# Attention and expert router on one core: the first pair of heads prepared in two halves, an overflow region moved into a product, the last product in two column parts

## The chip, the cores and the metric

The kernel runs on one core of a Trainium2 chip. The metric is the device time of one execution in microseconds (us); the number given for a kernel is the median of its runs. TensorE (PE in the profile) multiplies, VectorE (DVE), ScalarE (ACT) and GpSimd (POOL) work on elements, SyncE (SP) issues DMAs. Each engine executes its own instructions in order, and waits on semaphores for the others.

## The reference

There are two blocks, and the second takes the output of the first.

```python
# attention: q, k, v are (4, 8, 768, 64), centroids (8, 16, 64)
q_assign = argmax(normalised q . normalised centroids)      # 16 clusters
k_assign = argmax(normalised k . normalised centroids)
mask = q_assign[..., :, None] == k_assign[..., None, :]
scores = where(mask, q @ k.T / 8, -1e9)
x = softmax(scores) @ v                                     # then (3072, 512)
# router: expert_emb (8, 512), w1 (8, 512, 1024), w2 (8, 1024, 512)
logits = normalised x @ normalised expert_emb.T / tau
e = argmax(logits); gate = softmax(logits)[e]
out = gate * (relu(x @ w1[e]) @ w2[e])                      # each row by its own expert
```

## The kernel before

**Attention.** The 4 x 8 heads are taken as 16 pairs of heads (`NP`), with the two heads of a pair side by side in 128 partitions. A pair has 12 units: two halves of the queries (`hq`) by six blocks of 128 keys (`j`). `scores` (L497) makes a unit's scores in psum in two parts. Part 1 is the f32 product of `kT` and `qT`; part 0 is a bf16 product of the one-hot table `hot` (`t["H"]`), which adds a large negative number where the clusters differ. `expo` (L526) is ScalarE's exponential into one of six `prob` buffers, and `attend` (L531) multiplies by v and lets VectorE add up the sums. In the loop over units (L1441) TensorE scores two units ahead of the two that it attends.

Each pair is prepared by pieces (L365). "turn" brings q and k into the layout with the head's columns in partitions; "products" multiplies by the centroids (L411) and VectorE transposes the result (L420); "choose" finds the first best cluster with four VectorE instructions (L429 to L432); "codes" writes signed numbers into `cd`; and the table is `cd` transposed. For later pairs the turning is VectorE's and the table is made by a DMA transpose, all while an earlier pair is attended. For the first pair there is nothing to hide behind: `begin` (L327) does the turning on TensorE (L382) with evictions by ScalarE and VectorE (L388, L392), makes the table by twelve TensorE transposes (L466), and fills TensorE with matmuls on ones, `keep_up` (L229), ahead of the first data (ten) and ahead of the table (six). The order of every engine's instructions is the order of the program text; nothing is reordered by a scheduler.

The first loads: ScalarE's queue takes the centroids and the first half of k, SyncE's queue takes q, the rest of k, the embeddings `emb` and `tau`, then v in eight pieces, then the next pair. GpSimd makes the constants (identities, iotas, the zeros of `cd`). `unit_experts` and `turned_experts` scale and transpose `emb`.

**Experts.** After routing, 20 items are worked off: four "early", then "block" (128 rows) and "sized" (all rows of one expert up to a capacity) in turn; `later` holds all but the early ones, and `LAST` is the last of them. A block is `hidden` (L1299, two halves of 512 columns, w1) and `result` (L1318, w2, 16 matmul records of 512 columns in two halves of the contraction), an eviction by ScalarE into one of three buffers `y`, and a scatter by GpSimd. A sized item is `sized_hidden` and `sized_result`. Weights sit in two slots; the next w1 or w2 for a slot is loaded by SyncE when the slot's product is done. Gathers and scatters are queued as jobs and issued by `pump` and `share` in between. Every relu of `hidden` and `sized_hidden` is ScalarE's, in program order with the evictions of y.

`overflow` (L1589) is a region that runs only if some expert's rows exceed all the places planned (`n_used > KX`, L1605). With these inputs it is not taken, but each engine branches at it and adds the counts that the region's work would have added to its semaphores. Before, it stands ahead of item LAST-1:

```python
for i, it in enumerate(later):
    if i == LAST - 1:
        overflow()
        weights1(later[LAST])
        weights2(later[LAST])
```

Of the kernel before, what the change touches and what calls it, by code (L numbers as in the profile page):

```python
# [39 lines left out]
def kernel(  # L40
# [143 lines left out]
    def load(n, names):  # L184
        b, hp = pairs[n]
        t = ld.setdefault(n, {})
        for nm in names:
            x = t[nm] = ldp.tile([P, NJ, 2, D], F32, tag=nm + "32", name=nm + "32")
            for h in range(2):
                rows = {"q": q, "k": k, "v": v}[nm][b, 2 * hp + h]  # L190
                if nm == "v":

                    r = rows.rearrange("(i j a t) d -> a i t j d", i=2, a=2, t=SQ)
                    for g in range(P // SQ):
                        nc.sync.dma_start(
                            out=x[SQ * g : SQ * g + SQ, :, h], in_=r[g // 2, g % 2]
                        )
                    continue
                if n == 0:

                    for i in range(1 + (nm == "k")):
                        js = slice(NJ // 2 * i, NJ // 2 * i + NJ // 2) if nm == "k" else slice(0, NJ)
                        queue = nc.scalar if nm == "k" and i == 0 else nc.sync
                        queue.dma_start(
                            out=x[:, js, h], in_=rows.rearrange("(j p) d -> p j d", p=P)[:, js]
                        )
                    continue


                for w in range(D // SQ):  # L210
                    p0 = D * h + SQ * w
                    nc.sync.dma_start(
                        out=x[p0 : p0 + SQ].rearrange("p j h (o i) -> p (j h o) i", i=SQ),
                        in_=rows.rearrange("(s t) d -> t s d", t=SQ)[:, :, SQ * w : SQ * w + SQ],
                    )
# [36 lines left out]
    def constants():  # L252
        nc.vector.memset(onesb, 1.0)
        keep_up(10, idle_ps[:, 0])
        nc.vector.memset(epsc, EPS)
        make_identity(nc, ident)
        nc.gpsimd.iota(io_i, pattern=[[1, P]], base=0, channel_multiplier=0)

        nc.gpsimd.iota(
            tok_i.rearrange("p (b j) -> p b j", j=NJ),  # L260
            pattern=[[S, B], [P, NJ]],
            base=0,
            channel_multiplier=1,
        )
        for i, (p0, w) in enumerate(((0, -BIG), (D, -2.0))):
            nc.gpsimd.memset(wcd[p0 : p0 + D], w)
        make_identity(nc, identb)
        nc.gpsimd.memset(cd, 0.0)
        for i, (p0, c) in enumerate(((0, -BIG), (D, -1.0))):
            nc.gpsimd.memset(cd[p0 : p0 + D, :, :, 2 - 2 * i : 3 - 2 * i], c)  # L270
        make_upper_triangular(nc, sltb, val=1.0, diag=False)
        for prob in probs:
            nc.gpsimd.memset(prob[:, :, HS:HE], EPS)
        nc.gpsimd.memset(gate_p, 0.0)
        nc.vector.memset(cnB, 0.0)
        nc.vector.memset(ones, 1.0)
        nc.vector.memset(embT, 0.0)
        nc.vector.memset(cumx[:, 0], 0.0)
        nc.vector.tensor_copy(io_b, io_i)
        nc.vector.tensor_copy(io_f, io_i[:, 0:SQ])  # L280
        nc.vector.tensor_scalar(prefc, io_b[:, 0:C], -1.0, float(C), ALU.mult, ALU.add)
        nc.vector.tensor_scalar(prefe, io_b[:, 0:E], -1.0, float(E), ALU.mult, ALU.add)
# [17 lines left out]
    def unit_centroids():  # L300
        unit_rows(cn_r)
        nc.vector.tensor_scalar(cn2, bc(c_sb, [P, 2, D], 1), cn_r, None, ALU.mult)
        bk = misc()
# [8 lines left out]
    def unit_experts():  # L312
        unit_rows(en_r)
        nc.vector.reciprocal(tau, tau)
        nc.vector.tensor_scalar(emb, emb, en_r, tau, ALU.mult, ALU.mult)

    def turned_experts():
        bk = misc()
        for c in range(KD):
            nc.tensor.transpose(  # L320
                bk[:, E * c : E * c + E], emb[:, P * c : P * c + P], ident[0:E, 0:E]
            )
        nc.vector.tensor_copy(
            embT[:, :, 0:E], bk[:, 0 : KD * E].rearrange("p (c e) -> p c e", e=E)
        )

    def begin():  # L327

        nc.scalar.dma_start(out=c_sb, in_=centroids.rearrange("h c d -> (h c) d"))
        load(0, "q")  # L330
        load(0, "k")
        nc.sync.dma_start(out=emb, in_=moe_expert_emb)
        nc.sync.dma_start(out=tau, in_=moe_tau.to_broadcast([E, 1]))
# [4 lines left out]
        nc.scalar.activation(en_r, epsc[0:E], ACTF.Sqrt)  # L338
        norm_rows(cn_r, c_sb, P)
        unit_centroids()  # L340
        piece(0, "turn0")
        piece(0, "turn1")
        norm_rows(en_r, emb, E)

        nc.scalar.activation(cn_r, epsc, ACTF.Exp)
        piece(0, "products")
        for m in range(2):
            scores(m, (1,))
        un[2]["s_ps"] = psO.tile([P, 2, 512], F32, tag="o_ps", name="s_ps2")
        scores(2, (1,))  # L350
        piece(0, "choose")
        piece(0, "codes")
        keep_up(6, misc())
        unit_experts()
        rest = piece(0, "turn_numbers")
        next(rest)
        for m in range(3):
            scores(m, (0,))
        next(rest, None)
        turned_experts()  # L360
        for m in (0, 2, 1):
            expo(m)
        token_numbers()

    def prep_pieces(n):  # L365
# [8 lines left out]
        def turn(nm, half):  # L374
# [12 lines left out]
            if nm == "q":  # L387
                (nc.vector.tensor_copy if half else nc.scalar.copy)(  # L388
                    t["qT"][:, HS * half : HS * half + HS], bk[:, 0:HS]
                )  # L390
            else:
                (nc.scalar.copy if half else nc.vector.tensor_copy)(  # L392
                    in_halves(t["kT"])[:, half], bk[:, 0:HS].rearrange("p (s t) -> p s t", t=SQ)
                )
# [27 lines left out]
        def choose():  # L422
# [3 lines left out]
            amax = smp.tile(shp[0:2], F32, tag="amax", name="amax")  # L426
            sel = smp.tile(shp, BF16, tag="sel", name="sel", bufs=1)
            pm = smp.tile(shp[0:2], BF16, tag="pm", name="pm")
# [6 lines left out]
        def codes():  # L435
            pm = t["pm"]
            nc.scalar.activation(cd[..., 1], pm, ACTF.Copy, scale=wcd)
            for i, p0 in enumerate((0, D)):
                g = slice(p0, p0 + D)
                if n == 0:  # L440
                    nc.vector.scalar_tensor_tensor(
                        out=cd[g, :, :, 2 * i],
# [6 lines left out]
                    continue  # L449
# [4 lines left out]
            if n > 0:  # L454
                nc.sync.dma_start_transpose(
                    out=t["H"], in_=cd.rearrange("p s h c -> p (s h c)")
                )

        def turn_numbers():

            U = S // (4 * SQ)
            bks = []
            for half in range(2):
                bk = misc().bitcast(BF16)
                for u in range(U):
                    nc.tensor.transpose(  # L466
                        bk[:, P * u : P * u + P],
                        cd[:, U * half + u].rearrange("p h c -> p (h c)"),
                        identb,
                    )  # L470
                bks.append(bk[:, 0 : P * U].rearrange("r (s x) -> r s x", x=P))
            H = [t["H"][:, U * half : U * half + U] for half in range(2)]
            nc.vector.tensor_copy(H[0][:, :, 0:SQ], bks[0][:, :, 0:SQ])
            nc.scalar.copy(H[0][:, :, D:], bks[0][:, :, D:])
            nc.vector.tensor_copy(H[1][:, :, 0:SQ], bks[1][:, :, 0:SQ])
            yield
            nc.vector.tensor_copy(H[1][:, :, SQ:], bks[1][:, :, SQ:])  # L477
            nc.vector.tensor_copy(H[0][:, :, SQ:D], bks[0][:, :, SQ:D])

        return {  # L480
            "turn0": lambda: turn_blocks("q") if n else (turn("q", 0), turn("q", 1)),
            "turn1": lambda: turn_blocks("k") if n else (turn("k", 0), turn("k", 1)),
# [3 lines left out]
            "turn_numbers": turn_numbers,  # L486
# [10 lines left out]
    def scores(i, parts=(0, 1)):  # L497
# [10 lines left out]
        for part in parts:  # L508
            if part == 0:
                l = t["H"][:, 2 * j : 2 * j + 2, D:]  # L510
                r = t["H"][:, :, SQ * hq : SQ * hq + SQ]
            else:
# [786 lines left out]
    def hidden(it, halves=(0, 1)):  # L1299

        d = mo[it]
        for half in halves:
            if half == 0:
                d["hT"] = mop.tile([P, F], F32, tag="hT", name="hT")
# [12 lines left out]

    def result(it, halves=(0, 1)):  # L1318
        d = mo[it]
        for half in halves:  # L1320
            if half == 0:
                d["y_ps"] = bank("y_ps", psY)
# [55 lines left out]
    def between(n, it):  # L1378
        b, nb = divmod(n, NHP)
        if n == 0:  # L1380
# [6 lines left out]
            elif it == 3:  # L1387
                later_constants()
        elif it == 0 and n > 1:
# [49 lines left out]
    with tc.manual_schedule(engines=by_hand):  # L1439
        begin()  # L1440
        for i in range(0, len(units), 2):  # L1441
# [8 lines left out]
            for m in range(i + 2 if i else 3, min(i + 4, len(units))):  # L1450
                scores(m)
                expo(m)
                if it == 2 and m == i + 2:
                    piece(n + 1, "codes")
            between(n, it)
# [12 lines left out]
            for m in range(i, i + 2):  # L1468
                attend(m)
            if it == 2:  # L1470
# [10 lines left out]
            if it == 0:  # L1481
# [107 lines left out]
        def overflow():  # L1589
            n_used = nc.values_load(used[0:1, 0:1], min_val=0, max_val=KX + NO)  # L1590
            slot = later[-1].slot

            def more(j0, n):
                for j in range(j0, j0 + n):
                    it = Item("whole", KX + j, slot, more_tables)
# [9 lines left out]
            with tc.If(n_used > KX):  # L1605
# [12 lines left out]
                with tc.If(n_used > KX + MORE[0]):  # L1618
                    more(MORE[0], MORE[1])
                    with tc.If(n_used > KX + MORE[0] + MORE[1]):  # L1620
                        more(MORE[0] + MORE[1], MORE[2])

# [5 lines left out]
        for i, it in enumerate(later):  # L1628
            if i == LAST - 1:
                overflow()  # L1630
# [24 lines left out]
            elif i < LAST:  # L1655
# [10 lines left out]
                result(it)  # L1666
# [5 lines left out]
            else:  # L1672
# [3 lines left out]
                result(it)  # L1676
# [43 lines left out]
```

## Time and profile before

| | us |
|---|---|
| median of three runs (694.60 to 694.82) | 694.73 |
| the profiled execution: its own time | 695.09 |
| its span, first to last instruction | 693.3 |
| TensorE busy in the span | 684.1 |
| first exponential starts at | 14.61 |
| TensorE's work of the last product | 680.62 to 687.65 |
| last eviction of y, last scatter issued at | 687.69, 688.65 |

The mean granted clock of TensorE is 0.999 of full speed. Times inside the profile count from the start of the span. A line of a timeline gives the start, the duration, the engine, the source line and the operation with its tiles and shapes, and in brackets how long the engine had been idle and who released it. A line of the waits gives who waited for whom, the total, how often, and the longest. Matmul ends are modelled, and an f32 matmul appears as two records.

### The profile page before, as it was taken

To read this page: it belongs to the slowest core of one execution; us is meant where nothing else is said; L and a number is where in the kernel's file an instruction comes from. 1 tells how busy PE (TensorE), PEld (TensorE's weight loads), DVE (VectorE), ACT (ScalarE), POOL (GpSimd) and SP (SyncE) were. 2 spreads that over 40 slices of the span, in tenths; PEclk is the share of its full clock that TensorE was granted. 3 is DMA by queue.
4 is the path that set the end of the run, shared out by engine and by line. 5 is a ranking of instruction groups with operands and counts; after the bars stand their busy time and mean duration, and the time that the engine had idled before them with its cause. 6 is when DMAs were issued, how large, how long until landed. Compare 5 with 4: busy or idle time off the path is not lost.

```text
span 693.3 us, 16291 instructions
## 1 busy us (share of the span) xinstructions
PE 684.1 (99%) x6517; PEld 459.3 (66%) x6517; DVE 381.8 (55%) x667; ACT 262.6 (38%) x443; POOL 266.2 (38%) x494
## 2 busy tenths in 40 slices
PE   8999999999999999999999999999999999999996
PEld 4444444444444444455866778888979797979694
DVE  5789898999989999988564122140211303030310
ACT  5666665577656765576224120101010111111111
POOL 2122221321232212343315343576656465646502
PEclk9999999999999999999999999999999999999999
DMA  8755556875577588699699957457777686879450
GB/s 133 123 93 105 101 94 95 155 144 103 106 138 157 99 163 162 182 261 271 176 318 359 353 211 269 136 182 283 281 273 279 205 301 228 301 256 315 155 225 32
DMA packets 244157, 135.55 MB, mean 196 GB/s; under 512 B 207840, under 2 KB 207842, under 8 KB 244076
## 3 DMA queue, kind: packets, MB, share of 16 engines
q1 hardware_dynamic: 237116, 121.10, 64.3%
q0 software_dynamic: 6016, 13.12, 5.4%
q8 instruction: 54, 0.88, 0.6%
q10 hardware_dynamic: 944, 0.23, 0.2%
q14 instruction: 27, 0.22, 0.1%
HBM read 115.92 MB, written 13.12 MB: 186 GB/s over the span
## 4 chain that ended last, share of the span: by engine, by line
PE 91%; issue 3%; DMA 3%; POOL 1%; DVE 1%; POOLq 0%; ACT 0%; DVEq 0%
PE s_ps L518 22%; PE o_ps L540 18%; PE h_ps L1309 10%; PE y_ps L1325 10%; PE h_ps L1220 9%; PE y_ps L1258 6%; PE misc L1258 5%; PE x_ps L1220 3%; DMA out_dram<-ys,spidx 3%; PE misc L590 2%; PE misc L411 2%; PE misc L669 1%; PE idle_ps L232 1%; POOL xin L1078 0%; POOL out_dram L1089 0%
## 5 line engine op out<-in xcount | busy, mean ns | idle before, releaser
L529 ACT ACTIVATE prob<-s_ps 128x768 f32<-128x768 f32 x192 | 154.1, 814 | 100.7 <-PE s_ps L518 99.7
L518 PE MATMUL s_ps<-qT,kT 64*64 64x384 f32 x1536 | 155.6, 482 | 0.0
L540 PE MATMUL o_ps<-prob,v 64*64 64x385 f32 x1536 | 141.1, 483 | 0.0
L559 DVE TENSOR_TENSOR acc<-acc,prob 128x768 f32<-128x768 f32 x128 | 121.7, 951 | 8.5
L540 PEld LDWEIGHTS o_ps<-prob,v 64*64 64x64 f32 x1536 | 58.1, 133 | 65.2 <-issue 57.6
L1309 PE MATMUL h_ps<-xTm,w1s 128*128 128x128 f32 x768 | 88.5, 275 | 0.0
L1309 PEld LDWEIGHTS h_ps<-xTm,w1s 128*128 128x128 f32 x768 | 87.5, 192 | 1.4 <-issue 1.0
L1267 DVE STREAM_TRANSPOSE ys<-y_ps 128x256 f32<-128x256 f32 (+4 forms) x16 | 6.2, 404 | 147.0 <-PE y_ps L1258 119.1
L1325 PE MATMUL y_ps<-w2s,hT 128*128 128x512 f32 x192 | 84.5, 593 | 0.0
L518 PEld LDWEIGHTS s_ps<-qT,kT 64*64 64x64 f32 x1536 | 55.2, 133 | 36.9 <-issue 32.3
L574 POOL COPY behind<-acc 1x1 f32<-1x1 f32 x30 | 6.7, 223 | 178.2 <-DVE acc L559 169.3
L1220 PE MATMUL h_ps<-xTs,w1s 128*128 128x272 f32 (+7 forms) x384 | 72.9, 346 | 1.1 <-ACTq L1605 1.1
L1220 PEld LDWEIGHTS h_ps<-xTs,w1s 128*128 128x128 f32 x384 | 66.6, 190 | 8.0 <-issue 2.4
L1316 ACT ACTIVATE hT<-h_ps 128x512 f32<-128x512 f32 x24 | 14.3, 596 | 149.1 <-PE h_ps L1309 121.5
L1089 POOL DMA_INDIRECT out_dram<-ys,spidx x56 | 56.2, 1004 | 35.5 <-DVE ys L1282 18.3
L518 PE MATMUL s_ps<-hot 64*64 64x384 bf16 x768 | 64.2, 325 | 1.0 <-DVE hot L477 0.7
L1078 POOL DMA_INDIRECT xs<-x_rows,gpidx x56 | 56.9, 1016 | 18.7 <-issue 18.1
L1325 PEld LDWEIGHTS y_ps<-w2s,hT 128*128 128x128 f32 x192 | 35.6, 190 | 40.2 <-issue 39.9
L518 PEld LDWEIGHTS <-hot 64*64 64x64 bf16 x768 | 23.8, 106 | 43.9 <-issue 41.8
L1258 PE MATMUL misc<-hTs,w2o 128*128 128x272 f32 (+7 forms) x256 | 48.2, 346 | 0.0
L1258 PE MATMUL y_ps<-hTs,w2o 128*128 128x272 f32 (+7 forms) x256 | 48.0, 346 | 0.0
L1258 PEld LDWEIGHTS misc<-hTs,w2o 128*128 128x128 f32 x256 | 44.4, 190 | 2.7 <-issue 0.2
(274 smaller groups left out, 711.0 us busy)
## 6 DMA issues: line engine op xcount, KB each, us to landing
w1s<-in_moe_w_dram SPq DMA_DIRECT2D x18, 2048.0 KB
w2s<-in_moe_w_dram SPq DMA_DIRECT2D x18, 2048.0 KB
v<-in_v_dram SPq DMA_DIRECT2D x128, 48.0 KB
k<-in_k_dram SPq DMA_DIRECT2D x62, 96.0 KB
q<-in_q_dram SPq DMA_DIRECT2D x60, 96.0 KB
x_rows<-xb SPq DMA_DIRECT2D x60, 96.0 KB
xr<-x_rows SPq DMA_DIRECT2D x9, 512.0 KB
w1s<-in_moe_w_dram SPq DMA_DIRECT2D x4, 1024.0 KB
```

Of the source, the lines that this page charges most:

```text
L411: nc.tensor.matmul(bk[2 * C * i : 2 * C * i + 2 * C, 0:HS], lhsT=cnB[:, hp], rhs=r, start=True, stop=True,)
L518: nc.tensor.matmul(s_ps[D * half : D * half + D, h, 0:HS], lhsT=l[rows, half], rhs=r[rows], start=part == (1 if len(parts) < 2 else 0), st ...
L529: nc.scalar.activation(d["prob"][:, :, 0:HS], d["s_ps"][:, :, 0:HS], ACTF.Exp, scale=scale)
L540: nc.tensor.matmul(g["o_ps"][D * h : D * h + D, half, 0:HE], lhsT=ld[n]["v"][keys, j, h], rhs=d["prob"][keys, h, 0:HE], start=(j == 0), st ...
L559: nc.vector.tensor_tensor(g["acc"], g["acc"], d["prob"][:, :, 0:HS], ALU.add)
L1078: nc.gpsimd.indirect_dma_start(out=to, out_offset=None, in_=of, in_offset=bass.IndirectOffsetOnAxis(ap=at, axis=0), bounds_check=n - 1, oo ...
L1089: inst = nc.gpsimd.indirect_dma_start(out=to, out_offset=bass.IndirectOffsetOnAxis(ap=at, axis=0), in_=of, in_offset=None, bounds_check=n - 1,
L1220: nc.tensor.matmul(bk, lhsT=w1s[it.slot][:, c, P * f : P * f + P], rhs=d["xT"][:, c, 0:C], start=(c == 0), stop=(c == KD - 1),)
L1258: nc.tensor.matmul(bks[g][:, 0:C], lhsT=d["w2"][:, f, P * g : P * g + P], rhs=d["hT"][:, f, 0:C], start=(f == 0), stop=(f == KF - 1),)
L1309: nc.tensor.matmul(bk[:, m : m + P], lhsT=w1s[it.slot][:, c, f0 + m : f0 + m + P], rhs=d["xT"][:, P * c : P * c + P], start=(c == 0), stop ...
L1316: nc.scalar.activation(d["hT"][:, f0 : f0 + 512], bk, ACTF.Relu)
L1325: nc.tensor.matmul(bk, lhsT=d["hT"][:, P * c : P * c + P], rhs=w2s[it.slot][:, c], start=(c == 0), stop=(c == KF - 1),)
```

## The change

The first pair is prepared in two halves. Half 0 is the first 384 tokens of q and k, enough for units 0 to 2. Its four loads of 96 KB go over both SyncE's queue (head 0) and ScalarE's queue (head 1), those of half 1 over SyncE's; v of this pair is loaded in two pieces in natural order. `emb` and `tau` are loaded through GpSimd, after the first identity. `begin` runs turn, half product, choice, codes and table half by half, interleaved with the scores of units 0, 2 and 1; unit 3 is scored between the first two attends, and the choice product of pair 1 comes after units 4 and 5. Eight filler matmuls remain ahead of the first data, none ahead of the table. Scaling and evicting the embeddings moves to ScalarE, `token_numbers` into pair 0's fifth step. In the expert part, `overflow` moves between the two halves of the second product of block LAST-2; the region's items use that block's weight slot and other buffers, and the region reloads the second half of w2 at its end. The last block's second product is made in two column parts, 384 and 128, each evicted on its own.

```diff
-    def load(n, names):
+    def load(n, names, halves=(0, 1), queue=nc.sync):
...
+                if n == 0:
+                    x_h, rows = x[:, :, h], rows.rearrange("(j p) d -> p j d", p=P)
+                    if nm == "v":
+                        nc.sync.dma_start(out=x_h, in_=rows)
+                        continue
+                    for half in halves:
+                        js = slice(NJ // 2 * half, NJ // 2 * half + NJ // 2)
+                        (queue if h else nc.sync).dma_start(out=x_h[:, js], in_=rows[:, js])
+                    continue
...
-        keep_up(10, idle_ps[:, 0])
+        keep_up(8, idle_ps[:, 0])
         nc.vector.memset(epsc, EPS)
         make_identity(nc, ident)
+        nc.gpsimd.dma_start(out=emb, in_=moe_expert_emb)
+        nc.gpsimd.dma_start(out=tau, in_=moe_tau.to_broadcast([E, 1]))
...
     def unit_experts():
-        unit_rows(en_r)
-        nc.vector.reciprocal(tau, tau)
-        nc.vector.tensor_scalar(emb, emb, en_r, tau, ALU.mult, ALU.mult)
+        nc.vector.tensor_scalar(en_r, en_r, 1e-6, tau, ALU.add, ALU.mult)
+        nc.vector.reciprocal(en_r, en_r)
...
+        for half in range(2):
+            load(0, "qk", (half,), nc.sync if half else nc.scalar)
         load(0, "v")
         load(1, "qk")
         constants()
...
+        nc.scalar.activation(cn_r, epsc, ACTF.Sqrt)
         norm_rows(cn_r, c_sb, P)
+        norm_rows(en_r, emb, E)
         unit_centroids()
...
+        piece(0, "turn", "q", 0)(nc.vector.tensor_copy)
+        piece(0, "turn", "k", 0)(nc.scalar.copy)
+        turned_centroids()
+        unit_experts()
+        nc.scalar.activation(emb, emb, ACTF.Copy, scale=en_r)
+        piece(0, "half_products", 0)
+        piece(0, "turn", "q", 1)(nc.scalar.copy)
+        ld[0]["c_ps"] = psS.tile([P, 2, 512], F32, tag="s_ps", name="c_ps")
+        piece(0, "turn", "k", 1)(nc.scalar.copy)
+        turned_experts()
+        junk = smp.tile([P, 1], F32, name="junk1", bufs=1)
+        nc.scalar.activation(junk, epsc, ACTF.Exp)
+        piece(0, "choose", 0)
+        piece(0, "codes", 0)
+        scores(0, (1,))
+        piece(0, "half_products", 1)
         un[2]["s_ps"] = psO.tile([P, 2, 512], F32, tag="o_ps", name="s_ps2")
         scores(2, (1,))
+        evicts = piece(0, "table", 0)
+        evicts[0](nc.vector.tensor_copy)
+        evicts[1](nc.scalar.copy)
+        scores(0, (0,))
+        expo(0)
+        piece(0, "choose", 1)
+        piece(0, "codes", 1)
+        scores(2, (0,))
+        expo(2)
+        scores(1, (1,))
+        evicts = piece(0, "table", 1)
+        evicts[0](nc.vector.tensor_copy)
+        evicts[1](nc.scalar.copy)
+        scores(1, (0,))
+        expo(1)
...
+        def half_products(half):
+            W = HS // 2
...
+            for i in range(4):
+                r = in_halves(t["qT" if i < 2 else "kT"])[:, i % 2]
+                nc.tensor.matmul(
+                    bk[2 * C * i : 2 * C * i + 2 * C, 0:W],
+                    lhsT=cnB[:, hp],
+                    rhs=r[:, W // SQ * half : W // SQ * half + W // SQ],
+                    start=True,
+                    stop=True,
+                )
...
+            nc.vector.transpose(t["asn"][:, W * half : W * half + W], bk[:, 0:W])
...
+                nc.gpsimd.tensor_scalar(to[..., 1], pm, wcd, None, ALU.mult)
...
+    def result_last(it):
+
+        d = mo.pop(it)
+        y = mop.tile([P, DM], F32, tag="y", name="y", bufs=3)
+        cols = [slice(0, DM - P), slice(DM - P, DM)]
+        for cut in cols:
+            bk = bank("y_ps", psY)
+            for c in range(KF):
+                nc.tensor.matmul(
+                    bk[:, cut],
+                    lhsT=d["hT"][:, P * c : P * c + P],
+                    rhs=w2s[it.slot][:, c, cut],
...
+            nc.scalar.activation(
+                y[:, cut], bk[:, cut], ACTF.Copy, scale=it.gates[:, it.col : it.col + 1]
+            )
+        scatter(out[:], it.tables[2][:, it.col : it.col + 1], y, N)
...
+            elif it == 4:
+                token_numbers()
...
+            if (n, it) == (0, 1):
+                piece(1, "products")
...
                 attend(m)
+                if m == 0:
+                    scores(3, (1,))
+                    scores(3, (0,))
+                    expo(3)
...
-            slot = later[-1].slot
+            own = later[-3]
...
+                own.e = expert_of(own)
+                load_part(w2s[own.slot], moe_w2, own.e, KF, 1, 2)
...
             if i == LAST - 1:
-                overflow()
                 weights1(later[LAST])
                 weights2(later[LAST])
...
-                result(it)
+                result(it, (0,))
+                if i == LAST - 2:
+                    overflow()
+                result(it, (1,))
...
                 hidden(it)
-                result(it)
+                result_last(it)
```

## The prediction

> **What bounds the kernel now.** I read the page from the top, then the chain of waits at the start, the waits around line 1605, and the timeline of the end.
>
> ```profile
> span 693.3 us, 16291 instructions
> PE 684.1 (99%) x6517; PEld 459.3 (66%) x6517; DVE 381.8 (55%) x667; ACT 262.6 (38%) x443; POOL 266.2 (38%) x494
> ```
>
> TensorE is busy for 684.1 of 693.3 us. Its 9.2 us of idleness lie in four places: 1.07 before the first matmul, about 1.4 in gaps between 5.5 and 18 us, 1.10 at line 1605, and 5.65 after the last matmul (687.65). From 30 to 490 us it has none, so time won at the start lasts to the end. Beside the idleness, TensorE does work at the start that no output needs. The chain of waits there (start, length, what):
>
> ```profile
> 1.07 4.45 PE idle_ps L232 x10
> ...
> 5.73 0.93 PE q_ps L382 x6
> ...
> 9.09 0.59 DVE asn L420
> ...
> 13.80 0.38 DVE hot L477
> ...
> 14.20 0.39 PE s_ps L518 x4
> ...
> 16.48 1.60 PE o_ps L540 x15
> 18.07 0.83 PE misc L411 x8
> ```
>
> The first stage is a serial path: load, turn, product, choice on VectorE (9.09 to 12.5), table, and only at 14.61 the first exponential. At 18.07 four units are scored and two attended; I call this the mark. What follows it is the same work before and after. In TensorE's timeline,
>
> ```profile
> 7.14 0.52 PE L382 MATMUL misc<-ident,k 128*128 128x128 f32 x3 [0.17 <-DMA k<-in_k_dram]
> 11.09 1.47 PE L232 MATMUL misc<-onesb 128*128 128x512 bf16 x6
> ```
>
> the first shows that the last part of k arrives just before 7.14, the second 1.47 us of filler while VectorE chooses. At line 1605 the waits of TensorE and SyncE, and the instructions of that line on GpSimd, are:
>
> ```profile
> PE h_ps L1220 <- ACTq L1605: 1.1, 1, 1.1
> SPq L1128 <- PEq L1605: 6.5, 1, 6.5
> ```
> ```profile
> L1605 POOLq EVENT_SEMAPHORE  x5: 17/43/43, 656.7 to 665.4; - x5
> L1605 POOLq INC_SWDGE_SEM  x1: 1230/1230/1230, 665.4 to 665.4; - x1
> ```
>
> TensorE stands 1.10 us because ScalarE first evicts y (0.69 us) and only then passes the region. SyncE issues the last expert's w1 as soon as TensorE is past. GpSimd stays in the region until 666.6: there it waits for every transfer it has issued.
>
> **What the skill says.** "TensorE: Matmul & The Clock Gate", Part 1: the array starts at half clock, and a free-running 3.4 us window of activity raises it. The trace agrees: turns follow 0.213 us apart up to 5.95 and 0.109 us apart from 6.15. "Runtime: NRT & Kernel Launch", Instruction fetch mechanics: a taken branch must fetch its target. The trace has 0.4 us (ScalarE, 655.5 to 655.9) to 0.9 us (VectorE, 643.0 to 643.9) from the branch to the next event. "DMA: Bandwidth & Descriptors", Issuing engines are not separate DMA queues: all issuers share 16 engines. Here the sharing is uneven: GpSimd's gather issued at 630.46 landed at 632.79, but those issued at 634.46 and 638.21, with weight loads in flight, took 6.1 and 6.3 us by the trace's landings.
>
> **Start.** Added: two load DMAs (q and k go as eight of 96 KB, not six), four matmuls in the choice product, five choice instructions, three code writes. Removed: 6 of 8 DMAs of v (5.25 us of SyncE's issue become about 1), eight filler matmuls, one table eviction. Moved: emb and tau from SyncE to GpSimd, expert scaling (0.53) and its eviction (0.19) from VectorE to ScalarE, token numbers (0.84) to a place where VectorE waits 2.83 us (before 29.45).
> 1. Loads. The bytes on each queue are as before. In the trace q of head 0 landed at 3.73 (192 KB on SyncE), ScalarE's two k parts at 4.53 and 6.26. After: q and k of head 0 by 3.7, q of head 1 by 4.5, k of head 1 by 6.2. The filler ends at 1.07 + 8 x 0.427 = 4.5, so q turns to 5.2 at the cold clock, then TensorE waits 1 us. k turns to 6.6, the centroids to 6.8, cnB copies (2 x 0.23) to 7.3. First half product from 7.35 (whole product before: 7.85).
> 2. ScalarE's norm of emb (0.95) stands ahead of the kT copy; free if emb lands by 5.7. GpSimd issues it at about 1.35. An unloaded GpSimd transfer takes 2.3 us (630.46), a loaded one 6.3: 3.7 to 7.6. I take 5.2, since loads of 256-byte packets are only just starting. Behind GpSimd's two DMAs (1.0 each, as its gathers) lie the iotas: VectorE's io_b moves from 1.55 to 3.7, and cn is ready at 5.2 instead of 5.0; hidden by k's arrival.
> 3. Half the choice: 384 columns take 0.55 to 0.58, 24 take 0.17, so 192 take 0.38 to 0.40: transpose 0.40, four steps 1.5, codes 0.55. Product to 7.8, codes ready at 10.35. GpSimd's code product is not in the trace: 0.2 (memset) to 0.85 (L576), beside 0.54 of VectorE: nothing.
> 4. Meanwhile TensorE turns the rest (0.33 + 0.33), experts 0.4, scores of unit 0 (0.65), second half product (0.45), scores of unit 2 (0.65): to 10.65. Table 0.4 to 11.05, ScalarE's eviction 0.48 to 11.55, first exponential at 11.8. ScalarE's table load (1.28) fits from 9.45 to 10.75.
> 5. Second half: choice 11.2 to 12.7, codes 13.25, table 13.7, eviction 14.2, exponential of unit 1 to 15.0. TensorE: unit 1 and attend 0 to 14.55, unit 3 to 15.35, attend 1 to **16.0**. The mark falls from 18.07 to 16.0: **-2.07**. The product of pair 1 (0.83) moves behind units 4 and 5; its codes are due at about 20.8, as unit 6 is.
> What can be lost: if the 1 us gap keeps the array cold through the next window, half-rate work adds 0.5 to 1.0; if emb lands at 7.6, the kT copy goes from 6.7 to 8.5, 1.9 later. What can be won: k at 5.6 gives 0.5. Ends: -2.6 to -0.2.
>
> **Region.** It now stands after eight of the block's sixteen matmul records: 647.85 + 3.51 = 651.36 in old times. TensorE must drain (0.22, as 654.88 to 655.1) and branch (0.4 to 0.9); I take 0.75 in all. ScalarE has nothing pending, so the 1.10 goes: without more, the stage gains 0.35, say 0.4. But the block's y eviction now follows the region. The region's items write the same three y buffers, so this eviction waits for counts that GpSimd adds when it leaves. Behind it in ScalarE's queue are the next item's relus; TensorE has four psum groups (4.45) before it needs the first. GpSimd's last scatter ahead of the region is issued at 652.97. Before, it landed at 655.14 in quiet; now SyncE issues w1 at 651.65, and its packets begin at 652.8 (before: issue 655.17, packets from 656.4). Landing: 655.1 unloaded, 659.2 as the loaded gathers, 662.3 as the y scatter (655.89 to 665.16). I take 658.5. Leaving takes 0.2 + 1.23, then y 0.69 and a relu 0.3 with handovers 0.2: the fifth group starts 2.6 after the landing, at 661.1, against 660.44 before: **+0.7**. Bounds: -0.4 (landing before 657.4) to +4.4. y's own scatter is issued later; nothing before the end waits for it. w1 is issued 3.5 us earlier, w2 as before, and 20 us of slack hide both. The other buffers of the region's items (hTs, psH, the reload of w2's second half) matter only in a branch that isn't taken; the waits that they put on TensorE end with ScalarE's and SyncE's passing, which come before its own.
>
> **Last product.** 512 columns cost 0.428 a record. Now 16 x 0.32 (384) + 16 x 0.114 (128, as L1309) = 6.95 against 6.85, +0.1. The eviction ahead of the final scatter falls from 0.69 to 0.29 (128x160 takes 0.30), -0.4. The scatter stays. **-0.3**; bounds -0.4 to 0.
>
> **Sum.** -2.07 + 0.7 - 0.3 = -1.7. The profiled execution took 695.09 (span 693.3 and 1.8 around it), 0.36 above the median of 694.73. So 693.4 for it, and 693.0 for the median.
>
> **Rivals.**
> - Region free: scatters land early or y doesn't wait. For it: the quiet landing took 2.2 us. Against: gathers beside loads took 6. -2.07 - 0.4 - 0.3 = -2.8: 691.9. With k earlier and shorter handovers 690.4.
> - Start eaten: emb late through GpSimd or a cold array. For it: loaded GpSimd transfers took 6.3 us; TensorE pauses 1 us. Against: at 1.35 hardly any packet flows. -0.3 + 0.7 - 0.3: about 694.8. That the split start does nothing is this case too.
> - Slower: y's eviction waits for GpSimd's scatter behind w1's packets. The price is 1:1 from a landing at 657.8; it outweighs the other parts from 660.2, and by 0.2% from 661.6. At 662.3: +4.4 - 2.07 - 0.3 = +2.0: 696.8.
>
> **Numbers.** Forecast 0.38, region free 0.30, start eaten 0.17, slower 0.15. A measurement of this kernel can tell about 0.2% (1.4 us) from no change. Faster: 0.7 of the forecast, nearly all of the second, a tenth of the third: 0.57. Same: 0.26. Slower: 0.17. The range of 690.4 to 696.2 reaches from a free region with a good start to most of the slow case.
>
> **What would show it.** The first exponential at 11.8 and the first pair-1 product near 17.6 with the mark before it; ScalarE's kT copy at 6.7 without a wait for emb; TensorE idle about 1 us between the turns of q and of k. In the region: no wait of TensorE over 0.9, and then a wait of ScalarE's y for GpSimd or a scatter, with TensorE's fifth group late. A final eviction of 0.3. I am wrong if the mark is after 17, or if y waits past 661.

## The result, and the profile after

| | median of the runs | lowest to highest | ratio to before |
|---|---|---|---|
| before | 694.61 us | 694.39 to 694.82 | |
| changed | 691.75 us | 691.62 to 692.07 | 0.9959 (0.9949 to 0.9969) |

In this comparison the change makes the kernel 2.86 us faster (0.4%); the forecast was 1.7 faster. A later run of the same changed kernel gave a median of 693.9, and before 694.69 beside it: there the gain is nearly gone. The experiments below trace both numbers to the moment at which one of ScalarE's instructions starts. Below, the medians count three single executions far above the others (796, 1025 and 1855 us, of three kernels) and one of before (2553); the ratios leave them out, and without them only one median moves noticeably, 697.7 to 697.4.

The profiled execution of the changed kernel took 691.79, with a span of 690.0. From its page:

```profile
span 690.0 us, 16327 instructions
PE 681.5 (99%) x6533; PEld 460.5 (67%) x6533; DVE 382.5 (55%) x668; ACT 264.3 (38%) x447; POOL 268.3 (39%) x498
```

**The start.** TensorE's timeline (start, length, line, what, count, and in brackets how long the engine stood idle before it and for whom):

```profile
6.67 0.36 PE L435 MATMUL misc<-qT,cnB 128*32 128x192 f32 x2 [0.69 <-ACT kT L398]
...
11.43 0.52 PE L554 MATMUL s_ps<-hot 64*64 64x384 bf16 x8 [0.57 <-ACT hot L508]
...
13.22 0.49 PE L502 MATMUL misc<-identb,cd 128*128 128x128 bf16 x6 [0.62 <-DVE cd L475]
...
15.29 0.82 PE L576 MATMUL o_ps<-prob,v 64*64 64x385 f32 x8
...
17.65 0.52 PE L415 MATMUL misc<-qT,cnB 128*32 128x384 f32 x2
```

The mark, the end of the second attend, is at 15.29 + 0.82 = 16.11, where before had 18.07: 1.96 won. Three short waits are left in the path. Two copies end just before the first of them does, one on ScalarE and one on VectorE:

```profile
5.30 0.63 ACT L242 ACTIVATE junk<-emb 8x512 f32<-8x512 f32 x1 [0.98 <-DMA emb<-in_moe_expert_emb_dram]
...
6.17 0.45 ACT L398 COPY kT<-misc 128x384 f32<-128x384 f32 x1
...
11.84 1.51 ACT L565 ACTIVATE prob<-s_ps 128x768 f32<-128x768 f32 x2 [0.45 <-PE s_ps L554]
```
```profile
6.02 0.46 DVE L311 COPY cnB<-misc 64x64 f32<-64x64 f32 x2
```

ScalarE waits 0.98 us for the embeddings, and the copy of kT stands behind that wait in its queue. It ends at 6.62. But the half product needs cnB too, which VectorE completes at 6.48, so the embeddings' lateness costs at most 0.14 of the 0.69. The first exponential is at 11.84 (14.61 before).

**The region.** TensorE's waits from 540 us to the end are now a single line:

```profile
PE y_ps L1389 <- PEq L1677: 0.3, 1, 0.3
```

That is 0.3 in place of 1.1. ScalarE's timeline around the region, GpSimd's last scatter ahead of it, and GpSimd's leaving (instruction, count, ns of one, first and last start):

```profile
645.84 0.60 ACT L1356 ACTIVATE hT<-h_ps 128x512 f32<-128x512 f32 x1 [2.98 <-PE h_ps L1349]
653.29 0.69 ACT L1400 ACTIVATE y<-y_ps,slot_gates 128x512 f32<-128x512 f32 x1 [6.86 <-PE y_ps L1389]
```
```profile
648.60 0.97 POOL L1125 DMA_INDIRECT out_dram<-ys,spidx  x1 [0.30 <-issue]
```
```profile
L1677 POOLq INC_SWDGE_SEM  x1: 1215/1215/1215, 651.9 to 651.9; - x1
```

The scatter issued at 648.60 landed at 651.71, GpSimd left the region at 653.13, and y went at 653.29, just as its own product ended (653.20). So y waited for nothing that counts here, but the two ends were only 0.07 apart; the fifth group of the next item was on time. Between the hidden product of block LAST-2 (2.22 earlier than before) and the first product of the item after it (2.95 earlier) the region gained 0.73.

**The end.** ScalarE's two last evictions:

```profile
682.99 0.58 ACT L1373 ACTIVATE y<-y_ps,slot_gates 128x384 f32<-128x384 f32 x1 [4.62 <-PE y_ps L1366]
684.72 0.37 ACT L1373 ACTIVATE y<-y_ps,slot_gates 128x128 f32<-128x128 f32 x1 [1.15 <-PE y_ps L1366]
```

and the one of before:

```profile
687.69 0.69 ACT L1336 ACTIVATE y<-y_ps,slot_gates 128x512 f32<-128x512 f32 x1 [4.65 <-PE y_ps L1325]
```

The one on the path is 0.37 (0.69 before), so the lead grows from 2.97 at the end of the product to 3.29 at the end of the eviction.

### The profile page after: what moved, and what is told of

It is laid out like the page before. It is cut to its first block, busy times and chain, and to the rows that moved or that the text cites. A ratio compares the mean times of both kernels' runs of the same rounds, so it can differ in the third digit from the quotient of the medians.

```text
span 690.0 us, 16327 instructions
## 1 busy us (share of the span) xinstructions
PE 681.5 (99%) x6533; PEld 460.5 (67%) x6533; DVE 382.5 (55%) x668; ACT 264.3 (38%) x447; POOL 268.3 (39%) x498
## 4 chain that ended last, share of the span: by engine, by line
PE 89%; issue 5%; DMA 3%; POOL 1%; POOLq 0%; DVE 0%; ACT 0%; DVEq 0%
PE s_ps L554 23%; PE o_ps L576 18%; PE h_ps L1349 10%; PE y_ps L1389 10%; PE h_ps L1256 9%; PE misc L1294 5%; PE y_ps L1294 5%; PE x_ps L1256 3%; DMA xin<-x_rows,gpidx 2%; PE misc L626 2%; PE misc L415 1%; PE misc L705 1%; DMA emb<-in_moe_expert_emb_dram 1%; POOL out_dram L1125 0%; POOL xs L1114 0%
## 5 line engine op out<-in xcount | busy, mean ns | idle before, releaser
L1389 PE MATMUL y_ps<-w2s,hT 128*128 128x512 f32 x176 | 77.7, 593 | 0.3 <-PEq L1677 0.3
L1389 PEld LDWEIGHTS y_ps<-w2s,hT 128*128 128x128 f32 x176 | 32.5, 190 | 37.4 <-issue 37.4
```

The lines of the kernel that those rows point to most:

```text
L1389: nc.tensor.matmul(bk, lhsT=d["hT"][:, P * c : P * c + P], rhs=w2s[it.slot][:, c], start=(c == 0), stop=(c == KF - 1),)
```

## The experiments

All kernels of one group ran on one chip, a different chip for each group (the first comparison's chip isn't on record), beside the kernel before, which gave 694.57, 694.62 and 694.69. The theory at the outset: the three parts add up, and what the region costs is set by when y may go, which is when GpSimd has left.

### The parts by themselves

Start alone: the loads, the two halves and the embeddings' queue, with the old region and the old last product.

> The first pair's part of the change alone; region and last product as before. Theory (the three parts add up, the start moves the mark by 1.96 us as in the trace of the changed kernel, and nothing of it is given back before the expert stage): 2.0 us faster than before, mark at 16.1. Rival (the parts aren't independent, or a part of the gain between 30 and 640 us comes from elsewhere): the time differs from that by over 0.5 us, say 1.3 or 2.8 faster.

Measured: 692.58, ratio 0.9971 (0.996 to 0.9982), 2.0 faster. The profiled execution took 693.19 and has the mark at 16.68, 0.6 later than expected: in it the array turned warm, that is went from half to full clock, at 6.69 and not at 5.63, and the half product began at 7.25 and not at 6.67.

Region alone:

```diff
-                result(it)
+                result(it, (0,))
+                if i == LAST - 2:
+                    overflow()
+                result(it, (1,))
...
             if i == LAST - 1:
-                overflow()
```

> The moved region alone. Theory (TensorE loses 0.3 us at the region in place of 1.10, and y's eviction is released by GpSimd just when the product ends): 0.8 us faster than before. Rival (in this kernel ScalarE's relu comes late as in the trace of before, so the last two scatters are issued 2 us later against the product and y is held): no gain or up to 0.7 slower, with TensorE's fifth psum group of the next item late.

Measured: 693.80, ratio 0.9988 (0.9982 to 0.9995), 0.8 faster. Its trace shows the wait of y already at work, but harmless (ScalarE's timeline; the releaser named is GpSimd's scatter):

```profile
655.59 0.69 ACT L1364 ACTIVATE y<-y_ps,slot_gates 128x512 f32<-128x512 f32 x1 [7.34 <-DMA out_dram<-ys,spidx]
```

The product ended at 655.02 and GpSimd left at 655.37. y goes 0.57 late; TensorE, with four groups of work, notices nothing.

Last product alone:

```diff
-                result(it)
+                result_last(it)
```

> The last product in two column parts alone. Theory: TensorE pays 0.1 more, the eviction ahead of the last scatter falls from 0.69 to 0.37, so 0.3 us faster. Rival (the extra weight loads of the narrow part show, or the end is set by the scatter's landing whatever its start): 0.0 to 0.1 slower.

Measured: 694.44, ratio 0.9999 (0.999 to 1.0008). That is 0.13 faster by the medians and not to be told from nothing; the eviction in its trace is 0.37, as in the changed kernel.

The three make 2.0 + 0.8 + 0.1 = 2.9, and 2.86 was measured together in the first comparison: as far as two groups can be compared, the parts don't disturb each other.

### GpSimd made late

```diff
+                    for _ in range(6):
+                        nc.gpsimd.memset(cd, 0.0)
                     overflow()
```

> The changed kernel with six memsets of cd (1.38 us each, 8.3 us in all, nothing reads the result) on GpSimd just ahead of the region. Theory (y's eviction waits until GpSimd has left the region): GpSimd leaves about 7.5 us later than in the changed kernel, near 660; y starts then instead of at 653.3; TensorE has cover until its fifth psum group at 657.4, so the time is 3 us longer than that of the changed kernel (2 to 4). Rival (y waits for the product alone): no change against the changed kernel, 2.9 us faster than before.

Measured: 697.27, ratio 1.0039 (1.0025 to 1.0053), 5.5 over the changed kernel's 691.75 of the first comparison, and so above the 2 to 4 expected. GpSimd left at 659.64, y went at 659.80. TensorE's timeline:

```profile
660.74 5.19 PE L1256 MATMUL h_ps<-xTs,w1s 128*128 128x160 f32 x24 [3.35 <-ACT hTs L1263]
```

The gap of 3.35 is the wait. The other term is the 5.19: the same 24 matmuls take 3.53 in the run with five memsets below, and for 3.413 us from 660.742 the records give the clock as 0.5. Gap and half clock make 3.35 + 1.66 = 5.0; the spans differ by 5.1.

The same six memsets, with a buffer of its own for the items inside the region:

```diff
-                y = mop.tile([P, DM], F32, tag="y", name="y", bufs=3)
+                own_y = it.kind == "whole"
+                tag, n = ("yo", 1) if own_y else ("y", 3)
+                y = mop.tile([P, DM], F32, tag=tag, name=tag, bufs=n)
```

> The changed kernel with GpSimd kept busy ahead of the region by six memsets of 1.435 us (as in the run before, which gave 697.27), but the blocks' y tiles have a buffer of their own, so that no activation after the region takes the buffer that one of GpSimd's scatters still holds. Theory (what waits for GpSimd is the y eviction alone, through its buffer): the eviction goes at the end of its product, the fifth group starts about 0.2 us after it, and the time is that of the changed kernel, 691.75, within 0.4; 692.1 if the last block's own scatter now reaches further into the tail. Rival (every engine waits for GpSimd at the end of the region, whatever the buffer): 697 again, and the region would be slow wherever GpSimd is late.

Measured: 692.14, ratio 0.9965 (0.9952 to 0.9978). GpSimd left later still, at 661.38, and y didn't wait for it (ScalarE's timeline):

```profile
653.32 0.69 ACT L1402 ACTIVATE y<-y_ps,slot_gates 128x512 f32<-128x512 f32 x1 [5.31 <-PE y_ps L1389]
```

So the wait of y comes from the shared y buffer, and nothing else in the region held TensorE up when GpSimd was late.

Five memsets in place of six, shared buffer:

> The changed kernel with five memsets ahead of the region in place of six, shared buffer as in the changed kernel. GpSimd then leaves the region 1.43 us earlier than in the run with six (659.64 there), about 658.2 on the clock of that trace; the y eviction goes at 658.35, the fifth group's first relu some 0.6 after, and TensorE's gap ahead of it is about 1.9 to 2.2 us in place of 3.35. Theory[...]: no half clock in this trace, and 693.6, between 693.3 and 694.0 (1.9 over the changed kernel, and 3.6 under the run with six for 1.43 us less of waiting). Rival (the price is one for one throughout, and what else was lost came from elsewhere): 695.8, 1.43 under the run with six.

Measured: 696.84 (695.37 to 697.54). The expectation failed at its first step: in this group GpSimd came to the memsets later (last scatter issued at 649.98, not 648.43), so that it left at 659.75, no earlier than with six. But the two now make a pair with the same gap. TensorE's timeline of the profiled execution, which took 695.37:

```profile
660.85 3.53 PE L1256 MATMUL h_ps<-xTs,w1s 128*128 128x160 f32 x24 [3.31 <-ACT hTs L1263]
```

There is no half clock after this gap of 3.31, and it cost 3.6 over the changed kernel's profiled execution, about one for one. The six times of this kernel lie in two places, 695.4 and 695.7, and 696.8 to 697.5; the distance is near that of the half clock above (1.66). The mean granted clocks agree: 0.998 and 1.0 for the two, 0.996 to 0.997 for the four, and 0.995 to 0.997 for the kernel with six memsets. A gap of 3.3 is thus on the edge, and the clock falls in some executions; of the four no trace was kept, so for them that is an inference.

### The embeddings on another queue

```diff
-        nc.gpsimd.dma_start(out=emb, in_=moe_expert_emb)
-        nc.gpsimd.dma_start(out=tau, in_=moe_tau.to_broadcast([E, 1]))
...
             load(0, "qk", (half,), nc.sync if half else nc.scalar)
+        nc.sync.dma_start(out=emb, in_=moe_expert_emb)
+        nc.sync.dma_start(out=tau, in_=moe_tau.to_broadcast([E, 1]))
         load(0, "v")
```

> The changed kernel with the embeddings and tau issued on SyncE's queue, behind half 1's q and k loads and ahead of v, where half a start of the kernel before had them in turn, in place of GpSimd's queue. In the changed kernel they landed at 5.28 and 5.81, and ScalarE's first step waited for the first. Theory (the start's chain runs through the embeddings): they land at 6.9 to 7.3, the half product starts at about 8.3 in place of 6.67, the first exponential at 13.3 in place of 11.84, and the time is 693.4, between 692.8 and 693.9. Rival (the waits further on, where VectorE's steps set the pace, take up the lateness): the first exponential within 0.5 of 11.84 and 691.8 to 692.2.

Measured: 697.7, ratio 1.004 (1.0027 to 1.0053). Both theories missed. TensorE's timeline, and then busy time by stretch (its bounds and length; busy us of PE, PEld, DVE, ACT and POOL with counts; granted clock; DMA), this kernel's two lines first and the changed kernel's after them:

```profile
8.38 0.36 PE L435 MATMUL misc<-qT,cnB 128*32 128x192 f32 x2 [2.19 <-ACT kT L398]
```
```profile
6.00:9.30 3.30, 1.11 (x14) 0.62 (x13) 1.05 (x5) 2.00 (x5) 0.00 (x0) 1.00 1.29 198
9.30:19.50 10.20, 9.63 (x72) 4.17 (x74) 5.65 (x18) 5.61 (x10) 0.72 (x2) 0.50 1.53 142
```
```profile
6.00:9.30 3.30, 2.63 (x34) 1.48 (x34) 2.50 (x9) 2.87 (x8) 0.68 (x10) 1.00 1.29 177
9.30:19.50 10.20, 9.01 (x124) 4.00 (x120) 6.84 (x16) 6.49 (x10) 0.72 (x2) 1.00 1.02 130
```

The half product is 1.70 late, as expected: ScalarE had the embeddings only at 7.01. But the array, busy for 1.11 of 3.30 us while it waited, then ran at half clock to 19.57, and attention is 5.31 late from there on. In this execution (699.16) a further 1.9 was lost at the region, where the last scatter landed at 662.0.

The cold case was the prediction's "start eaten", which the changed kernel escapes with 2.63 of 3.30 busy. To separate its two terms, ten filler matmuls were put into the wait, with the y buffer of its own to keep the region out of it:

```diff
+        keep_up(10, idle_ps[:, 0])
         piece(0, "half_products", 0)
```

> The own buffer, the embeddings and tau on SyncE's queue as in an earlier run (697.7; its trace: half product 1.70 late, then half clock from 9.33 to 19.57, and attention 5.31 late from then on), and ten matmuls of constants ahead of the half product, which keep TensorE busy over the 2.47 us in which it waited for the embeddings. Theory (of the 5.31, some 1.7 is the embeddings' lateness and 3.6 the half clock that the wait brought): no half clock, attention 1.7 to 2.3 late, and 693.6, between 693.2 and 694.3. Rival (the lateness itself grows through the chain of small steps, the clock being its companion): attention still over 4 late, 696 or more.

Measured: 693.77; the profiled execution, 693.24, has no half clock and attention 1.19 late against the changed kernel. That is less than the 1.7 to 2.3 expected, but here the embeddings came earlier than in the run above (ScalarE's timeline of both, that run first):

```profile
7.01 0.63 ACT L242 ACTIVATE junk<-emb 8x512 f32<-8x512 f32 x1 [2.69 <-DMA emb<-in_moe_expert_emb_dram]
```
```profile
6.38 0.63 ACT L242 ACTIVATE junk<-emb 8x512 f32<-8x512 f32 x1 [2.05 <-DMA emb<-in_moe_expert_emb_dram]
```

The half product is at 7.86, 1.19 late, and attention is late by the same 1.19: without a half clock the embeddings' lateness is passed on one for one. In the run above that was 1.70, which leaves 3.6 of the 5.31 for the half clock that the wait brought. The medians agree on the first part: 693.77 is 1.72 over the own buffer alone (692.05, below, same chip). So the theory and its split hold.

### The second half's maximum first

```diff
+        piece(0, "choose", 1, (0,))
         evicts[0](nc.vector.tensor_copy)
...
-        piece(0, "choose", 1)
+        piece(0, "choose", 1, (1,))
```

> The changed kernel with the second half's maximum (one VectorE reduction) taken ahead of the copy of the first table's part in program order, in the gap in which VectorE waits (0.63 us, from 10.17 to 10.80). Theory (what ends the start is VectorE's row of steps up to the first exponential, and the reduction is one of them): the first exponential 0.3 to 0.4 us earlier and 691.4, between 691.2 and 691.6. Rival (the copy that it is put ahead of is itself waited for, and what follows moves back by as much): no change, 691.6 to 692.0.

Measured: 693.27 (692.33 to 694.36), ratio 0.9981 (0.9973 to 0.9989), slower than either expectation. In the start the array turned warm at 6.79 (5.63 in the changed kernel), the half product came 0.41 late, and by the fourth exponential the lateness was gone: the reduction had won that much. In this execution, of 692.47, the loss lay at the region: the scatters landed up to 655.45, y went at 657.03, TensorE waited 0.25, and in all 0.5 went there. Most executions took longer (the median is 0.8 more), and none of those was traced. So this run says nothing on what the reduction is worth.

### The changed kernel again

By now several traces of kernels with the changed region had shown landings far later than the 651.7 of the first trace. The last group therefore had the changed kernel itself, and the own buffer without any delay.

> The changed kernel itself, beside the next three. In the runs so far GpSimd's last scatters before the region landed at different times (651.7 in the trace of the changed kernel, 655.5 and 662.0 in two later ones), and the y eviction went 4 and 9 us later for it. Theory (the eviction can be 3.4 us late before TensorE waits): 691.8 where the scatters land before about 655, and 692.2 to 693.0 in executions in which they land later. Rival (the changed kernel has no such executions, and the lateness belongs to the other edits): 691.6 to 692.1 in every one.

Measured: 693.9, ten of fourteen times from 693.19 to 694.92 and four from 696.65 to 697.98; ratio 1.0003 (0.9991 to 1.0015). By the median it is 0.8 faster than before, by all its times together not at all, and later than either expectation. The four have mean granted clocks of 0.993 to 0.997, the ten 0.998 to 1.0: as with the late memsets, a half clock after a longer wait is likely in them, but not shown. ScalarE, GpSimd and TensorE in the profiled execution (693.83):

```profile
648.34 0.60 ACT L1356 ACTIVATE hT<-h_ps 128x512 f32<-128x512 f32 x1 [4.99 <-remote]
658.39 0.69 ACT L1400 ACTIVATE y<-y_ps,slot_gates 128x512 f32<-128x512 f32 x1 [9.45 <-DMA out_dram<-ys,spidx]
```
```profile
651.10 0.97 POOL L1125 DMA_INDIRECT out_dram<-ys,spidx  x1 [0.30 <-issue]
```
```profile
659.32 3.53 PE L1256 MATMUL h_ps<-xTs,w1s 128*128 128x160 f32 x24 [1.25 <-ACT hTs L1263]
```

Against the first trace, read in order: the block's second relu comes 2.05 us after its product (0.04 there), though the product itself is only 0.5 later. GpSimd's pacing copy, a single element that it reads from that relu's output so as to keep step, and the two scatters behind it are 2.5 later. Now they meet w1's 2 MB, which SyncE issues at 649.88. The DMA's busy tenths from 638 to 660 us, in slices of 0.55, first trace first:

```profile
DMA  9999999993300312100310869999999999699999
```
```profile
DMA  9999999999330300313000157899999999999999
```

The row of nines that begins at 651.2 in the first and at 652.3 in the second is w1 and then w2. In the first trace the scatter of 648.60 is ahead of it and lands at 651.71, after 3.1 us. Here the one of 651.10 lies in it and lands at 656.81, after 5.7. Then GpSimd leaves (658.22), y goes, a relu, and TensorE's fifth group, 2.5 us after the landing.

> The changed kernel with a buffer of its own for the y tiles inside the region, and nothing else. The y eviction then never waits for GpSimd's leaving. Theory: 691.7, between 691.5 and 692.1, and less spread than the changed kernel beside it; where that one reads 692.2 or more, this one stays. Rival (the region costs nothing in the changed kernel as it is): both within 0.15 of each other.

Measured: 692.05 (691.82 to 692.34), ratio 0.9962 (0.9949 to 0.9975). GpSimd is as late as beside it, and ScalarE's y doesn't care:

```profile
L1679 POOLq INC_SWDGE_SEM  x1: 1215/1215/1215, 657.0 to 657.0; - x1
```
```profile
653.48 0.69 ACT L1402 ACTIVATE y<-y_ps,slot_gates 128x512 f32<-128x512 f32 x1 [5.16 <-PE y_ps L1389]
```

The buffer of its own is worth 1.85 us on this chip; 1.5 of it is seen at the region in the two traces. It is the version to take: by the medians 2.6 faster than before here, where the changed kernel has 0.8, and 692.14 even with GpSimd held up.

> The run before, and the second half's maximum taken ahead of the copy of the first table's part, as in an earlier run (693.27, where the trace showed the first product of attention 0.41 late from transposes on a cold array, that lateness gone by the third exponential, and 0.5 lost at the region). Theory (the reduction ahead gains 0.35 to 0.45 in the start, and what hid it was the array's late warming and the region): 691.3, between 691.0 and 691.7, that is 0.3 to 0.4 under the own buffer alone. Rival (the start's later waits take it back): equal to the own buffer alone within 0.15.

Measured: 692.0, ratio 0.996 (0.9947 to 0.9973): equal to the own buffer alone. The start did gain 0.28 (fifth exponential at 16.54, not 16.82), but the lead was gone by 557 us; in the last stretch before that TensorE has one wait of 0.2 for instruction issue. That is one profiled execution; the rival's number came true, for a reason that isn't its own.

## Why the prediction was right, and where it was mis-sized

The forecast of -1.7 lies between the two comparisons, -2.86 and, by the medians, -0.8. Its mechanisms were those that the runs show; that the number fell between the two is partly luck, as follows.

**The start, -2.07: right (-1.96 by the trace, -2.0 alone), by errors that cancelled, which is luck.** k of head 1 landed at 4.99, not 6.2: the sum had carried before's arrival over to loads in a new order. That moved the half product from the predicted 7.35 to 6.67. The embeddings landed at 5.28 (5.2 was taken); ScalarE stood 0.98 for them, not hidden since k was so early, but cnB set nearly the same time, so at most 0.14 was lost. The lead of 0.68 was then used up in steps that had been taken too short: 3.69 and not 3.30 from the half product to the table, 1.48 and not 1.15 from there to the first exponential, which stood at 11.84 against 11.8. What can be lost was priced as bounds: 1.9 for late embeddings, and 0.5 to 1.0 for a cold array. With the embeddings on SyncE's queue the runs show 1.7 for the first, lost one for one, and 3.6 for the second. That bound was far too low: it reckoned with one further window, and the half clock lasted 10.24, three times the 3.413 seen after the later gap.

**The region, +0.7: the mechanism right, the landing mis-sized for the first comparison.** TensorE's 1.10 went, and 0.3 took its place (0.75 was allowed for drain and branch). y did become dependent on GpSimd's leaving, through the y buffers; the late memsets and the own buffer show it. The term that failed is "I take 658.5" for the last scatter. It came from the trace of before, in which the second relu is 2.2 us late (ScalarE's timeline):

```profile
650.21 0.60 ACT L1316 ACTIVATE hT<-h_ps 128x512 f32<-128x512 f32 x1 [5.13 <-remote]
```

The scatters are then issued late and, with w1 issued earlier, beside its packets. Set by the start of the block's second product (647.85 before, 645.64 in the first trace, 646.13 in the repeat), the landing was 651.71 + 2.21 = 653.9 in the first trace and 656.81 + 1.72 = 658.5 in the repeat. So where the relu is late, the number fits, with the 2.5 or 2.6 from the landing to the fifth group, though it had been picked from a range of 655.1 to 662.3; the region then gives 0.33 + 1.25 - 1.10 = +0.5. Where the relu is prompt, the rival "region free" is what happens, and the result of 691.75 is that rival's 691.9.

**The price of 1:1 was too simple.** It holds in the execution with a gap of 3.31. With 3.35 and half clock it was 1.5 to 1. The Trainium skill's page "TensorE: Matmul & The Clock Gate", HAM oscillation, puts the limit for idle gaps at about 3.4 us, and its Part 1 calls the window free-running, of 3413 ns. The half clock of 3.413 us agrees; that nearly the same gap brought it in one execution and not in another is what a free-running window leads one to expect. But the drop at the start came with 1.11 us of work in 3.30, so in this case a gap didn't have to be wholly idle.

**The last product, -0.3:** -0.32 in the trace from product to eviction; alone it measured -0.13, inside its interval of nothing.

**What decided between the rivals** is when one relu goes, and what delays it stays open. In the first trace of the changed kernel and in the four of the first group, two of which have the old region, it is 0.03 to 0.04 after its product; in the trace of before and in all eight of the other two groups, 0.8 to 2.4. So the kernel's text doesn't decide it; the chip may have a part, since each of the three groups is of one kind. The lines above name its releaser as "remote" where it is late. The traces have more: the relu waits for one semaphore, which the last matmul of its product raises. In the first trace that semaphore moves at 645.81 and in the repeat at 648.32, 0.02 to 0.03 ahead of the relu each time, although TensorE had begun the next product at 646.13 in the repeat. So ScalarE went as soon as the signal came, and the signal was late; no experiment went into why. Before's own time doesn't show it: its y eviction went ahead of the region, and its medians are 694.57 to 694.69 on all three chips.

## What to carry to other kernels

When a block of code is moved ahead of a tile's writer, look at which buffers the block writes too, even if its branch is never taken: the counts that it owes come when its slowest engine leaves, and a buffer of its own for the block takes the whole wait away. A step that rests on one transfer's landing should be priced for each order in which that transfer and the big loads beside it can start; one trace shows only one order. And a wait in the start, or one of about 3.3 us later on, can cost more than its length by the half clock that follows, so fill it or keep it short.

## What the runs showed of the hardware that was not expected

- 1.11 us of work in 3.30 brought TensorE to half clock for 10.24 us (9.33 to 19.57), although it was busy for 9.63 of 10.20 us in that stretch. At the later gap the half clock lasted 3.413.
- GpSimd's last scatter took 3.1 to 3.5 us from issue to landing in the three traces of the moved region with a prompt relu, where it was issued 0.7 to 0.8 us ahead of w1, and 5.7 to 6.8 in the eight with a late one. INC_SWDGE_SEM took 1.210 or 1.215 in each of these regions, whether GpSimd had waited long before it or not.
- The instant at which the array first turned warm moved between 4.16 and 6.79 us from execution to execution with the same eight filler matmuls ahead.
